# Float64 weights converted by VectorE alone, and a new order of the attention items behind each batch

## The chip, the cores and the metric

The kernel runs on one core of one Trainium2 chip. The metric is the device time of one execution in microseconds (us); the kernel before was timed three times. A core has five engines with a queue each: TensorE (PE, matmuls and transposes), VectorE (DVE), ScalarE (ACT), GpSimd (POOL) and SyncE (SP, which issues the DMAs). An engine works through its queue in order and waits on semaphores for what other engines and DMAs have to finish first.

## The reference

Three blocks in a row, for 8 batches, 576 tokens, width 512:

```python
def sm_attn(qq, kk, vv):                      # 8 heads of 64
    s = scale * np.matmul(qq, kk.transpose(0, 1, 3, 2))
    a = np.exp(s - np.max(s, axis=-1, keepdims=True))
    return np.matmul(a / (np.sum(a, axis=-1, keepdims=True) + 1e-09), vv)
p_packed = sm_attn(p, k, v)                   # 32 packed queries
x = sm_attn(q, p_packed, p_packed)            # heads joined to width 512
h = gelu_tanh(x @ w_in)                       # 512 -> 1024
u, v = h[..., :512], h[..., 512:]
v_s = np.einsum('ts,bsd->btd', w_sg, layer_norm(v) * g_ln) + b_sg
x = x + (u * v_s) @ w_out
# 4 experts of one head of 64 with causal softmax, the best 2 of 4 per token:
out = sum_over_chosen(w_e * (softmax(causal(x @ wq[e] @ (x @ wk[e]).T / 8)) @ (x @ wv[e]) @ wo[e]))
```

All is float32 but `w_in`, `w_sg` and `w_out`, which arrive as float64 and have to be made float32 by the kernel (a pair of 32-bit words per number).

## The kernel before, in words

The second packed softmax has only 32 columns per head, so its probabilities `a2` (256 columns and 576 tokens in two halves Q = 0, 1) stand for x, and the weights that follow are multiplied with the packed values once per batch (`wp` for `w_in`, `bdq` and `bdv` for the folded MoE weights). Products keep float32 accuracy by splitting both factors into a high and a low part (`a2h`, `a2l`; `wph`, `wpl`) and adding three products.

**The prologue** (about the first 125 us) loads and converts the weights (`from_f64`, L132), does the packed attention of batch 0 and folds `w_out` into the MoE weights (L257). A conversion handles 512 columns at a time: integer work on DVE (L137 to L139), the low word and the absolute value of the high word on ACT (L140, L141), a product and a sum on POOL (L142, L143), and the last select and product on DVE (L144). There are twelve such pieces: eight of `w_in` (two halves of four) and four of `w_out`. In the prologue a scheduler chooses the order of all engines.

**The main loop** takes about 112.7 us per batch. PE's order there is by hand, and only PE's: `front` holds the value tiles `v` (L519) and the gate tiles `u`, `back` the spatial products `vs` (L570), the MoE projections `qk` (L599, L604) and `vlog` (L629, L633), and, spread between them, the ten attention items of the batch before and the packed attention of the batch after. An item is a token tile and a pair of experts: S0 to S9 are its scores and softmax, T0 to T9 the transposes of the probabilities, y0 to y4 the products with the values, o0 to o4 the output tiles. S8 and S9 (`att_last`, L707 and L713) belong to the last 64 tokens and take two PSUM buffers each; T8 and T9 are at L744. The packed attention of the next batch goes through `pT`, `natT` (transposes of k and q, L326), `s` (L349; s1 is k against the packed queries, s2 is q against the packed values), `a1T`, `pp`, `ppT` (L401) and `split_a2` (L465 on ACT, L81 on POOL). A function `run` merges two lists of such steps by given costs. The other engines' orders follow from the scheduler's priorities.

PSUM has four buffers (`pd`), taken in turn: a product cannot start until the contents of the buffer four takes ago have been read by ACT or DVE. Of the buffers in SBUF the four of slot "C" matter here: `a2h` and `a2l` of the next batch take the places of those of this batch and so wait until the last `qk` product (L604) has read them.

Of the kernel before, what the change touches and what calls it, by code (L numbers as in the profile page):

```python
# [7 lines left out]
F32 = mybir.dt.float32  # L8
# [17 lines left out]
def packed_attention_mlp_moe_kernel(  # L26
# [39 lines left out]
    def slot(tag, dt=F32, w=None, name=None):  # L66
        t = sb.tile([P, BY[tag]], dt, tag=tag, name=name or ("s" + tag), bufs=NB[tag])
        return t if w is None else t[:, :w]
# [60 lines left out]
            nc.sync.dma_start(raw_in[f, j][64 * d:64 * d + 64],  # L129
                              src[j * P + 64 * a:j * P + 64 * a + 64, f * 1024:(f + 1) * 1024])  # L130

    def from_f64(raw, top, pw, dst):  # L132

        words = raw.rearrange("p (n t) -> p n t", t=2)
        lw, hw = words[:, :, 0], words[:, :, 1]
        low, in_range = lw.bitcast(F32), hw.bitcast(F32)
        nc.vector.tensor_scalar(top, hw, 3, 0x3FFFFFF8, op0=OP.logical_shift_left, op1=OP.bitwise_and)  # L137
        nc.vector.scalar_tensor_tensor(top, hw, -0x40000000, top, op0=OP.bitwise_and, op1=OP.bitwise_or)
        nc.vector.tensor_scalar(pw, top, -0x800000, None, op0=OP.bitwise_and)  # L139
        nc.scalar.activation(in_range, in_range, AF.Abs)  # L140
        nc.scalar.activation(low, lw.bitcast(U32), AF.Copy, scale=2.0 ** -52)  # L141
        nc.gpsimd.tensor_tensor(pw.bitcast(F32), low, pw.bitcast(F32), op=OP.mult)  # L142
        nc.gpsimd.tensor_tensor(pw.bitcast(F32), pw.bitcast(F32), top.bitcast(F32), op=OP.add)  # L143
        nc.vector.scalar_tensor_tensor(dst if dst is not None else low, in_range, LEAST_F64, pw.bitcast(F32),  # L144
                                       op0=OP.is_ge, op1=OP.mult)
        return low

    wst = {}

# [19 lines left out]

    def prep_w_in(f):  # L170
        t = w_tile(f"in{f}")
        for j in range(4):
            dst = t[:, j, :]
            from_f64(raw_in[f, j], dst.bitcast(I32), slot("t", I32, 512, name="pw"), dst)
        keep_w(f"in{f}")

    folded = {}
# [58 lines left out]
    def prep_w_out(c):  # L236

        wo = slot("p", w=512, name="wo")
        from_f64(raw_out[c], wo.bitcast(I32), slot("t", I32, 512, name="pw"), wo)
        pt = pd("woT")[:, 0, :]  # L240
        for j in range(4):
            nc.tensor.transpose(pt[:, j * P:(j + 1) * P], wo[:, j * P:(j + 1) * P], ident)
        t = slot("D", w=512, name="woT")
        act_copy(t, pt)
        woT[c] = t
# [50 lines left out]
    def p1_steps(b):  # L296
# [68 lines left out]
        def a1T(Q):  # L365
            a1 = s.pop(("a1", Q))
            pt = pd("a1T")[:, 0, :]
            for c in range(4):
                o = (c % 2) * HALF + (c // 2) * P
                nc.tensor.transpose(pt[:, c * P:(c + 1) * P], a1[:, o:o + P], ident)  # L370
            t = slot("t", w=512, name="a1t")
            nc.vector.tensor_copy(t, pt)
            r = small.tile([P, 2, 32], F32, name="a1r", bufs=1)
            for h in range(2):
                nc.vector.transpose(r[:, h, :], a1[:, h * HALF + 256:(h + 1) * HALF])
            s["a1T", Q] = (t, r)
# [80 lines left out]
    def split_a2(b, Q):  # L457
        s = ST[b]
        f = s.pop(("a2f", Q))
        hi, lo = slot("C", F32R, name="a2h"), slot("C", F32R, name="a2l")  # L460
        f = f.rearrange("p (a i) -> p i a", a=2)
        for o, i0, n in ((0, 0, S), (S, 256, 64)):
            src = f[:, i0:i0 + n // 2, :]
            dh, dl = (t[:, o:o + n].rearrange("p (i a) -> p i a", a=2) for t in (hi, lo))
            nc.scalar.activation(dh, src, AF.Copy)  # L465
            lo_part(nc.gpsimd, dl, src, dh)
        s["a2", Q] = (hi, lo)
# [44 lines left out]
    def v_tiles(b, cs):  # L512
        s = ST[b]
        pt2 = pd("v")
        for ci, c in enumerate(cs):
            n = 0
            for x, y in PASSES:
                for Q in range(2):
                    nc.tensor.matmul(pt2[:, ci, :], s["a2", Q][x][:, c * P:(c + 1) * P], wp_part(b, 1, y, Q),  # L519
                                     start=n == 0, stop=n == 5)  # L520
                    n += 1
        for ci, c in enumerate(cs):
            pt = pt2[:, ci, :]
            vg = slot("t", w=512, name="vg")
            nc.scalar.activation(vg, pt, AF.Gelu_apprx_tanh)
            st = small.tile([P, 6], F32, name="bnst")
            nc.vector.bn_stats(st, vg)
            mv = small.tile([P, 2], F32, name="mv")
            nc.vector.bn_aggr(mv, st)
            rstd = small.tile([P, 1], F32, name="rstd")  # L530
            nc.vector.tensor_scalar(rstd, mv[:, 1:2], LN_EPS, None, op0=OP.add)
            nc.gpsimd.tensor_tensor(rstd, rstd, mhalf, op=OP.pow)
            nc.vector.scalar_tensor_tensor(vg, vg, mv[:, 0:1], g_bc, op0=OP.subtract, op1=OP.mult)
            hi, lo = slot("B", F32R, 512, name="vnh"), slot("B", F32R, 512, name="vnl")
            nc.scalar.activation(hi, vg, AF.Copy, scale=rstd)
            if c < 4:
                nc.vector.scalar_tensor_tensor(lo, vg, rstd, hi.bitcast(F32), op0=OP.mult, op1=OP.subtract)
            else:
                nc.vector.scalar_tensor_tensor(hi[64:P], vg[64:P], rstd[64:P], hi[64:P].bitcast(F32),
                                               op0=OP.mult, op1=OP.subtract)  # L540
                nc.vector.memset(lo[64:P].bitcast(F32), 1.0)
                nc.scalar.activation(lo[:64], vg[:64], AF.Copy, scale=rstd[:64])
            s["vn", c] = (hi, lo)
# [4 lines left out]
    def u_tile(b, m):  # L548
        s = ST[b]
        u = slot("D", name="u")  # L550
        pt = pd("u")
        n = 0
        for x, y in PASSES:
            for Q in range(2):
                for h in range(2):
                    nc.tensor.matmul(pt[:, h, :HALF], wp_part(b, 0, y, Q)[:, m * P:(m + 1) * P],
                                     s["a2", Q][x][:, hs(h)], start=n == 0, stop=n == 5)
                n += 1
        nc.scalar.activation(two(u), pt[:, :, :HALF], AF.Gelu_apprx_tanh)
        s["u", m] = u  # L560
# [234 lines left out]
    def do(steps):  # L795
        for _, f in steps:
            f()
# [32 lines left out]
    def front(b, go):  # L830

        v_tiles(b, VT[0])
        v_tiles(b, VT[1])
        v_tiles(b, VT[2])
        go("T0")
        for m in range(4):
            u_tile(b, m)

    def back(b, go, extra=()):
        main = []  # L840

        def add(cost, fn, *a):
            main.append((cost, lambda: fn(*a)))

        go("S1")
        vs_tile(b, 0)
        go("T1 S3 y0")
        vs_tile(b, 1)
        go("T2 S5 o0 T3")
        vs_tile(b, 2)  # L850
        go("y1 T4 S6")
        vs_tile(b, 3)
        go("T5 o1 S7")
        bdw(b)
        weights(b + 1, ("in1", "in0"))
        nxt = attention(b)
        add(4.0, go, "y2 T6 S8")
        add(4.8, qk, b, 0)
        add(3.5, go, "T7 o2 S9")
        add(4.8, qk, b, 2)  # L860
        add(3.0, go, "y3 T8")
        add(2.7, go, "o3 T9")
        add(2.0, go, "y4")
        add(4.2, vlog, b, VT[0])
        add(1.0, go, "o4")
# [12 lines left out]
        nxt("S0 S2")
        if b + 1 == B:
            qk(b, 3)  # L880
            return nxt
        wp_mm(b + 1, 1)
        qk_mm(b, 3)
        wp_out(b + 1, 1)
        qk_out(b, 3)
        wprime(b + 1, 0)
        weights(b + 1, ("qk", "vg"))
        nxt("S4")
        return nxt

    P1 = {}
# [6 lines left out]

    first = p1_steps(0)
    do(first[:6])  # L900
    for j in range(4):
        load_raw_in(1, j)
    do(first[6:14])
    for c in range(4):
        load_w_out(c)
    for j in range(4):
# [26 lines left out]
    with tc.manual_schedule(engines={mybir.EngineType.PE}):  # L933
        ahead(1)
        go = back(0, attention(-1))
        for b in range(1, B):
            front(b, go)
            go = back(b, go)
        go("S4 S1 T0 S3 T1 y0 T2 S5 o0 T3 y1 T4 S6 o1 T5 S7 y2 T6 S8 o2 T7 S9 y3 T8 o3 T9 y4 o4")


# [29 lines left out]
```

## Time and profile before

| | |
|---|---|
| median of 3 runs | 1007.45 us (1006.8 to 1008.74) |
| profiled execution | 1005.63 us, span 1003.9 us |
| mean granted clock of TensorE | 0.948 |
| PE busy | 895.2 us, 89% |
| DVE / ACT / POOL busy | 57% / 47% / 12% |

PE is the busiest engine by far. Its busy time is a sum over 8009 matmul records, so the profile is read by the places at which PE stands still and by the stretches in which its granted clock is below 1.00: in the 40 slices of the page the clock is lowest in the second and third (0.7 and 0.5 of the full one), inside the prologue.

### The profile page before, as it was taken

The page shows a single profiled execution, that of the slowest core. Times are in us where ns is not written, and L with a number is a line of the kernel's source. Part 1 is how long each engine was busy: PE and PEld are TensorE (multiplying, and loading weights), DVE is VectorE, ACT ScalarE, POOL GpSimd, SP SyncE. Part 2 cuts the span into 40 slices and gives each one's busy share as a digit, 9 for nine tenths or more (in the row PEclk, how much of TensorE's full clock was granted, in tenths as well). Part 3 has the DMA queues.
Part 4 walks back from the last instruction along what each step waited for, and adds up shares of the span by engine and source line. Part 5 has one row for each costly group of instructions (what it writes and reads, how often), then busy time and mean ns, then how long its engine had stood idle before and what let it go on. Part 6 is the DMA issues. An engine that isn't in the chain of part 4 may idle for free.

```text
span 1003.9 us, 19707 instructions
## 1 busy us (share of the span) xinstructions
PE 895.2 (89%) x8009; PEld 747.2 (74%) x8009; DVE 568.5 (57%) x1354; ACT 475.8 (47%) x1087; POOL 119.9 (12%) x120
## 2 busy tenths in 40 slices
PE   3529899899998999899998999999989999899987
PEld 2205788697877888697877888787868788687965
DVE  3897433865367543865367543864377543865154
ACT  4423523465436452565436452655436452554245
POOL 0565010210012000210012000200012000200000
PEclk9758899999999999999999999999998999999989
DMA  8863133103230143103320132104320231100001
GB/s 234 201 205 131 43 114 119 65 11 124 94 95 22 46 143 92 64 12 124 101 88 22 55 137 90 64 12 142 98 93 2 77 107 40 64 11 23 17 11 37
DMA packets 60191, 81.07 MB, mean 81 GB/s; under 512 B 15107, under 2 KB 48387, under 8 KB 57029
## 3 DMA queue, kind: packets, MB, share of 16 engines
q1 hardware_dynamic: 60100, 79.81, 24.9%
q8 instruction: 63, 1.03, 0.4%
q14 instruction: 28, 0.22, 0.1%
HBM read 66.68 MB, written 13.12 MB: 79 GB/s over the span
## 4 chain that ended last, share of the span: by engine, by line
PE 54%; DVE 16%; ACT 7%; POOL 2%; issue 2%; POOLq 0%; ACTq 0%
PE vs L570 7%; PE o L774 6%; PE qk L599 5%; PE vlog L629 5%; PE v L519 5%; PE y L759 4%; PE aTp L731 3%; PE sc L684 3%; PE qk L604 3%; PE natT L326 3%; PE vlog L633 2%; DVE at L695 2%; ACT at L691 2%; PE sc L713 2%; DVE nm L687 2%
## 5 line engine op out<-in xcount | busy, mean ns | idle before, releaser
L599 PE MATMUL qk<-gh,w_qk 128*128 128x288 f32 x512 | 94.0, 306 | 2.1 <-DVE bdq L81 1.5
L691 ACT ACTIVATE at<-sc,nm 128x256 f32<-128x256 f32 (+3 forms) x128 | 66.1, 524 | 57.2 <-DVE nm L687 55.4
L570 PE MATMUL vs<-w_sg,vnh 128*128 128x288 f32 x512 | 91.7, 301 | 0.0
L599 PEld LDWEIGHTS qk<-gh,w_qk 128*128 128x128 f32 x512 | 76.5, 194 | 13.8 <-DVE nm L687 5.0
L78 ACT ACTIVATE aT<-aTp 128x512 f32<-128x512 f32 (+4 forms) x160 | 61.0, 436 | 52.5 <-PE aTp L731 47.3
L417 POOL TENSOR_TENSOR bt<-bt,mx 128x576 f32<-128x576 f32 x14 | 16.3, 1162 | 577.4 <-DVE gsm L662 531.6
L570 PEld LDWEIGHTS vs<-w_sg,vnh 128*128 128x128 f32 x512 | 74.5, 189 | 4.2 <-DVE yl L81 2.5
L629 PE MATMUL vlog<-w_vg,gh 128*128 128x260 f32 (+1 forms) x320 | 60.6, 287 | 0.0
L687 DVE TENSOR_REDUCE nm<-sc 128x2 f32<-128x256 f32 (+3 forms) x64 | 51.7, 819 | 12.3 <-PE sc L684 11.2
L759 PE MATMUL y<-aT,v 128*64 128x128 f32 (+2 forms) x960 | 58.1, 264 | 0.4 <-ACT aT L78 0.4
L695 DVE TENSOR_SCALAR at<-at,sm,gw 128x256 f32<-128x256 f32 (+3 forms) x128 | 55.9, 478 | 2.3
L599 PE MATMUL qk<-gl,w_qk 128*128 128x288 f32 x256 | 55.4, 298 | 0.0
L759 PEld LDWEIGHTS y<-aT,v 128*64 128x64 f32 (+1 forms) x960 | 46.9, 137 | 11.3 <-issue 5.4
L774 PE MATMUL o<-w_o,yh 128*128 128x512 f32 (+1 forms) x160 | 53.8, 418 | 1.4 <-ACT yh L762 1.4
L570 PE MATMUL vs<-w_sg,vnl 128*128 128x288 f32 x256 | 54.8, 295 | 0.0
L731 PE MATMUL aTp<-ident,at 128*128 128x128 f32 x320 | 47.9, 280 | 5.7 <-DVE at L695 5.7
L635 ACT ACTIVATE v<-vlog 128x512 f32<-128x512 f32 (+1 forms) x24 | 12.6, 524 | 83.4 <-PE vlog L633 83.4
L629 PEld LDWEIGHTS vlog<-w_vg,gh 128*128 128x128 f32 (+1 forms) x320 | 47.5, 178 | 2.2
L684 PE MATMUL sc<-qk 64*128 64x128 f32 (+3 forms) x384 | 47.6, 352 | 0.2 <-DVE qk L81 0.2
L731 PEld LDWEIGHTS aTp<-ident,at 128*128 128x128 f32 x320 | 37.5, 142 | 13.1 <-issue 7.0
L578 DVE TENSOR_TENSOR gt<-vs,u 128x576 f32<-128x576 f32 x32 | 24.1, 754 | 39.4 <-PE vs L575 39.4
L519 PE MATMUL v<-wph,a2h 128*128 128x512 f32 x80 | 32.2, 477 | 14.8 <-ACT a2h L465 14.8
(210 smaller groups left out, 2098.5 us busy)
## 6 DMA issues: line engine op xcount, KB each, us to landing
w_in<-kept_in SPq DMA_DIRECT2D x14, 1024.0 KB
k<-in_k_dram SPq DMA_DIRECT2D x32, 256.0 KB
v<-in_v_dram SPq DMA_DIRECT2D x32, 256.0 KB
q<-in_q_dram SPq DMA_DIRECT2D x32, 256.0 KB
w_qk<-kept_qk SPq DMA_DIRECT2D x8, 1024.0 KB
out_dram<-ot SPq DMA_DIRECT2D x32, 256.0 KB
w_vg<-kept_vg SPq DMA_DIRECT2D x8, 520.0 KB
raw_w_qk<-in_moe_w_in_dram SPq DMA_DIRECT2D x8, 256.0 KB
```

The costliest lines, as they stand in the source:

```text
L78: nc.scalar.activation(o, i, AF.Copy, scale=scale)
L519: nc.tensor.matmul(pt2[:, ci, :], s["a2", Q][x][:, c * P:(c + 1) * P], wp_part(b, 1, y, Q), start=n == 0, stop=n == 5)
L570: nc.tensor.matmul(pt[:, h, :HALF], s["vn", c][x][:, cols], w_sg[y][:, c, hs(h)], start=(c, x, y) == (0, 0, 0), stop=False)
L599: nc.tensor.matmul(o[:, h, :], W["w_qk"][y][:, m, cols], s["g", m][x][:, hs(h)], start=(m, x, y) == (0, 0, 0), stop=False)
L629: nc.tensor.matmul(pt[:n, ci, :260], s["g", m][x][:, c * P:c * P + n], W["w_vg"][y][:, m, :], start=(m, x, y) == (0, 0, 0), stop=False)
L684: nc.tensor.matmul(pt[:, e, :L], qs[x][r, j * P:L], ks[y][r, :L], start=False, stop=i == 2, skip_group_check=True)
L687: nc.vector.tensor_reduce(nm, pt[:, :, :L], axis=AX.X, op=OP.max, negate=True)
L691: nc.scalar.activation(ats[e][:, :L], pt[:, e, :L], AF.Exp, bias=nm[:, e:e + 1], accum_out=sm[:, e:e + 1])
L695: nc.vector.tensor_scalar(ats[e][:, :L], ats[e][:, :L], sm[:, e:e + 1], s["w"][:, j, 2 * pr + e:2 * pr + e + 1], op0=OP.mult, op1=OP.mult)
L731: nc.tensor.transpose(pt[:, e, c * P:c * P + P], ats[e][:, c * P:c * P + P], ident)
L759: nc.tensor.matmul(pt[64 * e:64 * e + 64, pr * w:pr * w + w], s["v2"][:m, c, col:col + D], s["aT", pr, e, j][c][:m, :], start=c == 0, stop ...
L774: nc.tensor.matmul(pt[:n, :], ys[x][:, pr * n:pr * n + n], W["w_o"][y][:, pr, :], start=i == 0, stop=i == 5)
```

## The change

It has three parts, and the order of PE's work is seen best in the rows further down.

- `from_f64` works on DVE alone, with seven instructions (L137 to L143 of the changed kernel). `w_in` is converted in pieces of 1024 columns, `w_out` in pieces of 512 as before. The scratch buffer `pw` of the wide pieces comes from slot "A".
- In the prologue the loads of q are put ahead of half of the raw `w_in`, those of v behind all of it, and batch 0 copies `a1T` by ACT.
- In the main loop S4 leaves the end of the batch and stands between o0 and y1; T1 goes behind the second `vs`, next to y0; S8 and S9 stand closer together behind the product of `qk` 0, whose evacuation comes after S8; `pp`, `ppT` and s2 of the next batch stand between the `vlog` tiles; `u` 0 goes ahead of T0. `split_a2` and the s2 step are issued under a higher priority of the scheduler.

```diff
-    def from_f64(raw, top, pw, dst):
+    def from_f64(raw, pw, dst):
...
-        low, in_range = lw.bitcast(F32), hw.bitcast(F32)
+        top, f, in_range = dst.bitcast(I32), pw.bitcast(F32), hw.bitcast(F32)
         nc.vector.tensor_scalar(top, hw, 3, 0x3FFFFFF8, op0=OP.logical_shift_left, op1=OP.bitwise_and)
         nc.vector.scalar_tensor_tensor(top, hw, -0x40000000, top, op0=OP.bitwise_and, op1=OP.bitwise_or)
         nc.vector.tensor_scalar(pw, top, -0x800000, None, op0=OP.bitwise_and)
-        nc.scalar.activation(in_range, in_range, AF.Abs)
-        nc.scalar.activation(low, lw.bitcast(U32), AF.Copy, scale=2.0 ** -52)
-        nc.gpsimd.tensor_tensor(pw.bitcast(F32), low, pw.bitcast(F32), op=OP.mult)
-        nc.gpsimd.tensor_tensor(pw.bitcast(F32), pw.bitcast(F32), top.bitcast(F32), op=OP.add)
-        nc.vector.scalar_tensor_tensor(dst if dst is not None else low, in_range, LEAST_F64, pw.bitcast(F32),
-                                       op0=OP.is_ge, op1=OP.mult)
-        return low
+        nc.vector.scalar_tensor_tensor(f, lw.bitcast(U32), 2.0 ** -52, f, op0=OP.mult, op1=OP.mult)
+        nc.vector.tensor_tensor(f, f, dst, op=OP.add)
+        nc.vector.tensor_scalar(hw, hw, 0x7FFFFFFF, None, op0=OP.bitwise_and)
+        nc.vector.scalar_tensor_tensor(dst, in_range, LEAST_F64, f, op0=OP.is_ge, op1=OP.mult)
...
-        go("T1 S3 y0")
+        go("S3")
         vs_tile(b, 1)
-        go("T2 S5 o0 T3")
+        go("T1 y0 T2 S5")
         vs_tile(b, 2)
-        go("y1 T4 S6")
+        go("T3 o0 S4 y1")
         vs_tile(b, 3)
-        go("T5 o1 S7")
+        go("T5 S6 o1 T4")
         bdw(b)
...
-        add(4.0, go, "y2 T6 S8")
-        add(4.8, qk, b, 0)
-        add(3.5, go, "T7 o2 S9")
+        qk_mm(b, 0)
+        go("y2 S7 S8")
+        qk_out(b, 0)
+        go("T6 S9")
+        add(2.0, go, "o2")
         add(4.8, qk, b, 2)
-        add(3.0, go, "y3 T8")
-        add(2.7, go, "o3 T9")
-        add(2.0, go, "y4")
+        add(2.9, go, "T7 y3")
+        add(2.2, go, "T8 o3")
+        add(3.1, go, "T9 y4")
         add(4.2, vlog, b, VT[0])
-        add(1.0, go, "o4")
-        add(4.2, vlog, b, VT[1])
-        add(2.1, vlog, b, VT[2])
-        add(0.0, gates, b)
...
-        for Q, (_, f) in enumerate(p1[cut:]):
-            f()
-            split_a2(b + 1, Q)
+        for Q in range(2):
+            if p1:
+                with tc.high_priority(offset=150):
+                    p1[cut + Q][1]()
+                    split_a2(b + 1, Q)
+            if Q == 0:
+                go("o4")
+                vlog(b, VT[1])
+        vlog(b, VT[2])
+        gates(b)
...
         weights(b + 1, ("qk", "vg"))
-        nxt("S4")
...
-        go("S4 S1 T0 S3 T1 y0 T2 S5 o0 T3 y1 T4 S6 o1 T5 S7 y2 T6 S8 o2 T7 S9 y3 T8 o3 T9 y4 o4")
+        go("T0 S1 S3 T1 y0 T2 S5 o0 T3 S4 y1 T5 S6 o1 T4 S7 y2 T6 S8 o2 T7 S9 y3 T8 o3 T9 y4 o4")
```

Three places in the instruction order follow. The first is PE from the last transposes of the packed values (`ppT`) to the first value product `v` of the next batch. Before:

```order
L633 MATMUL vlog<-bdv,a2l 64x260
L401 MATMUL ppT<-ident,pp_9788 128x128
L401 MATMUL ppT<-ident,pp_9865 128x128
L349 MATMUL s_9920<-qT,ppT 32x288 x8
L349 MATMUL s_9949<-qT,ppT 32x288 x8
...
L474 MATMUL wp<-w_in_9300,ppT 32x512 x8
...
L604 MATMUL qk<-a2l,bdq 128x288 x2
L474 MATMUL wp<-w_in_9302,ppT 32x512 x8
...
L684 MATMUL sc<-qk 128x384 x6
L519 MATMUL v<-wph,a2h 128x512 x2
```

After, from the same transposes (line numbers are three lower):

```order
L398 MATMUL ppT<-ident,pp_9703 128x128
L398 MATMUL ppT<-ident,pp_9772 128x128
L346 MATMUL s_9783<-qT,ppT 32x288 x8
...
L630 MATMUL vlog<-bdv,a2l 128x260
L346 MATMUL s_9861<-qT,ppT 32x288 x8
...
L630 MATMUL vlog<-bdv,a2l 64x260
...
L471 MATMUL wp<-w_in_9236,ppT 32x512 x8
...
L601 MATMUL qk<-a2l,bdq 128x288 x2
L471 MATMUL wp<-w_in_9238,ppT 32x512 x8
L516 MATMUL v<-wph,a2h 128x512 x2
```

The s2 products (`s<-qT,ppT`) moved from behind the last `vlog` tile to places between the tiles, and the scores of S4 (the 384 wide `sc`) no longer stand ahead of the first `v`.

The second place is PE from S8 to S9 of a batch (`sc` 64x288 x12 is one item; T6 and T7 are `aTp` x8). Before:

```order
L474 MATMUL bdv<-w_vg,ppT 32x260 x8
L759 MATMUL y<-aT,v_8314 64x128 x12
L731 MATMUL aTp<-ident,at 128x128 x8
...
L713 MATMUL sc<-qk 64x288 x12
L315 MATMUL pT<-ident,pn 128x128 x2
L326 MATMUL natT<-ident,k 128x128 x8
L328 MATMUL remT<-ident,kr 128x128
L599 MATMUL qk<-gh,w_qk_748 128x288 x2
...
L731 MATMUL aTp<-ident,at 128x128 x8
L774 MATMUL o<-w_o_948,yh 128x512
...
L713 MATMUL sc<-qk 64x288 x12
```

After:

```order
L601 MATMUL qk<-a2l,bdq 128x288 x2
L756 MATMUL y<-aT,v_8314 64x128 x12
...
L681 MATMUL sc<-qk 128x512 x6
...
L710 MATMUL sc<-qk 64x288 x12
L728 MATMUL aTp<-ident,at 128x128 x8
...
L710 MATMUL sc<-qk 64x288 x12
L771 MATMUL o<-w_o_904,yh 128x512
```

Between S8 and S9 there stood most of `qk`, a transpose of k, s1, T7 and o2; now T6 alone stands there, and the first product of `qk` 0 is ahead of both.

The third place is PE around s1 of the second half (Q = 1) and y3 (`y` x16 is y3). Before:

```order
L326 MATMUL natT<-ident,k 128x128 x8
L328 MATMUL remT<-ident,kr 128x128
L731 MATMUL aTp<-ident,at 128x128 x8
...
L604 MATMUL qk<-a2l,bdq 128x288 x2
L349 MATMUL s_9560<-kT,pT 32x288 x8
L326 MATMUL natT<-ident,q 128x128 x8
L328 MATMUL remT<-ident,qr 128x128
L759 MATMUL y<-aT,v_8314 64x128 x16
```

After:

```order
L323 MATMUL natT<-ident,k 128x128 x8
L325 MATMUL remT<-ident,kr 128x128
L346 MATMUL s_9503<-kT,pT 32x288 x8
L728 MATMUL aTp<-ident,at 128x128 x8
L756 MATMUL y<-aT,v_8314 64x128 x16
L323 MATMUL natT<-ident,q 128x128 x8
```

s1 of the second half now follows its own transposes of k directly, and y3 follows T7 directly, where two other steps stood in between.

## Rows read from the trace of the kernel before

**Rows 1.** Waits of PE from 130 us: total us, times, longest us.

```profile
PE v L519 <- ACT a2h L465: 14.8, 6, 2.5
PE sc L707 <- DVE yl L81: 8.6, 7, 1.2
PE sc L707 <- DVE bdq L81: 5.8, 7, 0.8
PE aTp L731 <- DVE at L695: 5.7, 8, 3.2
PE wp L474 <- DVE bt L411: 5.5, 6, 0.9
...
PE v L519 <- POOL a2l L81: 2.2, 5, 0.5
PE qk L599 <- DVE bdq L81: 1.5, 1, 1.5
```

**Rows 2.** Windows: us, busy us of PE, PEld, DVE, ACT, POOL, PEclk, DMA, GB/s.

```profile
406.00:411.00 5.00, 4.73 (x44) 3.92 (x44) 4.86 (x14) 3.32 (x10) 1.16 (x1) 1.00 0.47 162
420.00:425.00 5.00, 5.00 (x20) 4.07 (x19) 3.10 (x10) 2.07 (x4) 0.56 (x1) 0.82 0.00 0
465.00:470.00 5.00, 4.02 (x26) 3.33 (x26) 2.90 (x5) 2.96 (x7) 0.00 (x0) 0.66 0.65 237
685.00:690.00 5.00, 2.93 (x38) 2.38 (x39) 2.96 (x7) 3.69 (x10) 0.00 (x0) 1.00 0.90 324
```

**Rows 3.** Timeline of PE, a first v and an S8: start us, us, instruction.

```profile
419.43 1.06 PE L519 MATMUL v<-wph,a2h 128*128 128x512 f32 x2
...
421.91 0.62 PE L519 MATMUL v<-wph,a2h 128*128 128x512 f32 x2
...
466.31 1.70 PE L713 MATMUL sc<-qk 64*64 64x288 f32 x12
```

**Rows 4.** Timeline of POOL before the first v of that batch.

```profile
412.24 1.86 POOL L81 TENSOR_TENSOR a2l<-a2f,a2h 128x576 fp32r<-128x576 f32 x2 [2.55 <-ACT a2h L465]
```

**Rows 5.** Timeline of PE in the tail: y0 behind T1, S8, S9, y3.

```profile
969.89 0.86 PE L759 MATMUL y<-aT,v 128*64 128x128 f32 x4 [0.44 <-ACT aT L78]
...
985.29 1.00 PE L713 MATMUL sc<-qk 64*64 64x288 f32 x12
...
989.31 0.19 PE L707 MATMUL sc<-causal,identb 128*128 128x64 bf16 x1 [0.49 <-ACT at L719]
...
990.36 1.97 PE L759 MATMUL y<-aT,v 128*64 128x128 f32 x32
```

**Rows 6.** Timeline of ACT behind the transposes of k, Q = 1.

```profile
476.63 1.08 ACT L334 ACTIVATE kT<-natT 128x512 f32<-128x512 f32 x2 [1.02 <-PE natT L326]
477.61 0.75 ACT L358 ACTIVATE a<-s,st 128x576 f32<-128x576 f32 x1
```

**Rows 7.** Windows of the prologue, columns as in rows 2.

```profile
42.00:43.00 1.00, 0.21 (x1) 0.00 (x0) 1.00 (x4) 1.00 (x2) 0.00 (x0) 0.50 1.03 220
50.00:75.00 25.00, 5.44 (x22) 2.34 (x18) 24.45 (x30) 7.24 (x13) 16.73 (x13) 0.50 0.66 202
```

**Rows 8.** Timeline of DVE in the prologue.

```profile
42.55 0.38 DVE L139 TENSOR_SCALAR pw<-w_in 128x512 int32<-128x512 int32 x1
42.85 0.41 DVE L137 TENSOR_SCALAR w_in<-raw_w_sg 128x512 int32<-128x512 int32 x1
...
46.89 0.75 DVE L417 TENSOR_TENSOR bt<-bt,mx 128x576 f32<-128x576 f32 x1
...
48.84 0.68 DVE L138 SCALAR_TENSOR_TENSOR w_in<-raw_w_sg,w_in 128x512 int32<-128x512 int32 x1
...
51.14 1.48 DVE L139 TENSOR_SCALAR pw<-wo 128x512 int32<-128x512 int32 x1
```

**Rows 9.** Groups by line of DVE, prologue: busy us, mean ns, idle.

```profile
L139 DVE TENSOR_SCALAR pw<-w_in 128x512 int32<-128x512 int32 x8 | 7.4, 932 | 0.1
L144 DVE SCALAR_TENSOR_TENSOR w_in<-raw_w_sg,pw 128x512 f32<-128x512 f32 x4 | 5.8, 1491 | 2.7 <-POOL pw L143 2.7
```

More of the change, by code (lines that the diff above doesn't have):

```diff
@@ L171, in prep_w_in @@
         t = w_tile(f"in{f}")
-        for j in range(4):
-            dst = t[:, j, :]
-            from_f64(raw_in[f, j], dst.bitcast(I32), slot("t", I32, 512, name="pw"), dst)
+        for i in range(2):
+            from_f64(raw_hold[f][i][:, :2048], slot("A", I32, 1024, name="pw"),
+                     t[:, 2 * i:2 * i + 2, :].rearrange("p j n -> p (j n)"))
         keep_w(f"in{f}")
@@ L238, in prep_w_out @@
         wo = slot("p", w=512, name="wo")
-        from_f64(raw_out[c], wo.bitcast(I32), slot("t", I32, 512, name="pw"), wo)
+        from_f64(raw_out[c], slot("t", I32, 512, name="pw"), wo)
         pt = pd("woT")[:, 0, :]
@@ L371, in a1T @@
             t = slot("t", w=512, name="a1t")
-            nc.vector.tensor_copy(t, pt)
+            (nc.vector.tensor_copy if b else act_copy)(t, pt)
             r = small.tile([P, 2, 32], F32, name="a1r", bufs=1)
@@ L834, in front, with back @@
         v_tiles(b, VT[2])
+        u_tile(b, 0)
         go("T0")
-        for m in range(4):
+        for m in range(1, 4):
             u_tile(b, m)
-    def back(b, go, extra=()):
+    def back(b, go):
         main = []
@@ L900, in packed_attention_mlp_moe_kernel @@
     do(first[:6])
-    for j in range(4):
+    for j in range(2):
         load_raw_in(1, j)
-    do(first[6:14])
+    do(first[10:14])
+    for j in range(2, 4):
+        load_raw_in(1, j)
+    do(first[6:10])
     for c in range(4):
```

## The prediction

> **What bounds the kernel now.** PE is busy for 89% of the span, so I read first the waits of PE behind the prologue, then the windows in which its granted clock is under 1.00, then single places in the timeline, and last the prologue. The waits [rows 1] come back in every batch: the first value product `v` stands for `a2h` (14.8 us in 6 batches, up to 2.5) and then for `a2l` (2.2); S8 stands for PSUM buffers that hold `bdq` and `bdv` (8.6 and 5.8 in 7 batches); T1 for its probabilities (5.7, of which 3.2 in the tail); `wp` for s2's `bt` (5.5). The other engines are idle often enough; each wait is a short chain through ACT, DVE or POOL that PE reaches too early.
>
> A wait costs twice where the clock falls behind it. Behind the `a2h` wait the granted clock of the window is 0.82, behind one S8 it is 0.66, behind another S8 it stays 1.00 [rows 2]. In cycles this is one level against the other, 1.2 against 2.4 GHz: a pair of `v` products takes 1.06 us and then 0.62, S8's twelve matmuls 1.70 where the same ones in the tail take 1.00 [rows 3, 5]. The price of such a fall at `v`: from 419.43 to 421.91 are 2.48 us for three pairs that start 0.46 apart at full clock (estimate from 0.62 less the overlap of 0.16), so 2.48 - 1.38 = 1.1. At S8 it is 1.70 - 1.00 = 0.7. The trace has falls at all 6 `a2h` waits and, of the 7 S8, at 5.
>
> The prologue is another regime. From 50 to 75 us DVE is busy for 24.45 of 25 us and PE for 5.44 [rows 7]. There DVE decides when the weights are ready.
>
> **The change part by part.** Sums are made against the profiled execution, 1005.63 us, 1.73 above its span of 1003.9; the median of the runs is 1.8 above it.
>
> *1. s2 earlier, S4 gone from the end.* Both s2 now stand between the `vlog` tiles, the first some 9 us earlier than before, so that the chain `bt`, softmax, `a2f` is over long before `qk` 3 ends. The `wp` wait goes (5.5) and so do both `v` waits in their present form (14.8 + 2.2): 22.5 us. What is late next: `a2h` and `a2l` take the SBUF places that the last `qk` product has to release, and POOL then makes `a2l` of the first half in 1.86 [rows 4] before it starts the second. POOL started at 412.24; the large part of the second half (1.16, an estimate: the share of 1.86 that goes with 576 of the row's 576 and 64 columns, plus a fixed part) would be ready at 415.3. PE has the last `wp` (about 1.0) and two kinds of products to do from 412.2 on and wants it at about 414.4. So 0.9 stays, times 7 = 6.3. Gain 22.5 - 6.3 = 16.2. A stall of 0.9 is as long as the present `wp` wait, in whose window the clock stays 1.00 [rows 2], so I also count the clock, 6 x 1.1 = 6.6, of which I take 6.0 (one fall in eleven may stay). Bounds: nothing (the stall only moves) to 22.5 + 6.6 = 29.
>
> *2. S8 and S9.* S8 now comes when `bdq` and `bdv` have long been read, under `qk` 0. The 14.4 us go, with 5 x 0.7 = 3.5 of clock. Late next is S9, with only T6 in front of it. In the tail S8's matmuls begin at 985.29 and S9's second buffer is free at 989.31, after a wait of 0.49 in spite of o2 and T7 between [rows 5]: that is about 3.1 behind the last of S8's matmuls. T6 covers 1.1 of it, so S9 waits 2.0, 7 x 2.0 = 14.0, and if half of these waits also drop the clock, 7 / 2 x 0.7 = 2.5. Gain 17.9 - 16.5 = 1.4. Bounds: -10 (the exponentials of S8 stand behind the evacuation of `qk` 0 too) to +10.
>
> *3. T1 behind the second `vs`.* The steady part of its wait, 5.7 - 3.2 = 2.5, goes. But y0 follows T1 at once; the tail has that place, with 0.44 [rows 5]: 7 x 0.44 = 3.1. Net -0.6, bounds -3 and +2.5.
>
> *4. s1 of the second half directly behind its transposes.* ACT takes 1.08 for `kT` from the moment at which PE has finished them [rows 6]; T7 and o2 covered this, and now 7 x 1.1 = 7.7 is lost. Bounds 3 (the second of the two copies alone) and 11.
>
> *5. y3 directly behind T7.* ACT copies T7's result in two parts, 1.08 in all, and the exponential of s1 (0.75, and its sum read out) can stand between them [rows 6]. y3 takes 1.97 and its first half needs T6 alone [rows 5], which covers 0.98: 1.08 + 0.75 + 0.2 + 0.1 - 0.98 = 1.15, 6 batches, 6.9. y4 behind T9 is the smaller case, 6 x 0.25 = 1.5 (estimate: half of y0's). Together -8.4, bounds -13 and -2.
>
> *6. The first batch and the tail.* In the first batch there are no items between the steps of the packed attention; they follow each other at once and I count one `kT` and two exponentials, 2.6; its `qk` wait of 1.5 goes [rows 1]. In the tail the 3.2 of T1 goes with one fall of 1.1, and the scores of S1 with less in front of them give about 2 back (an estimate: its maximum and exponential as in a steady item, less one product): +2.3. Net +1.2, bounds -2 and +5.
>
> *7. Conversions.* The seven instructions cost per 512 columns 0.41 (as L137) + 0.68 (L138) + 0.38 (L139) + 0.68 + 0.67 (the sum: 0.75 x 512 / 576) + 0.41 + 0.68 = 3.9; the added three are 0.68 + 0.67 + 0.41 = 1.76, times 12 pieces = 21.1. What DVE gets back is the time it lost beside POOL: L139 took 0.38 at 42.55, with POOL idle, and 1.48 at 51.14 with POOL at work [rows 8]. On eight L139 that is 7.4 - 8 x 0.38 = 4.4 and on four L144 5.8 - 4 x 0.68 = 3.1 [rows 9], 7.5 on 12 of 48 instructions; at that rate all would give 30, and if the rest gave nothing, 7.5. So DVE's work changes by something between -9 and +14, and the pieces of 1024 save the start of four times seven instructions. With a value near the middle the last weight comes when it did, and the prologue costs 0.5 more: the folds and `v` behind it stay as they are. POOL and ACT, which lose 24 instructions each, were on this path only through DVE. The order of the loads moves SP's queue: q comes earlier and v of batch 0 later, both under conversion. Bounds -9 and +14 where PE follows DVE one to one.
>
> Whether POOL is the cause decides between these ends. The DMA queues were full at 42 to 43 us (share 1.03) while L139 was at its quick value, and less full (0.66) in the window of the slow one [rows 7], so the rows speak for POOL and against the loads. By the Trainium skill, GPSIMD Engine Reference, section 1 (Specifications), GpSimd shares its SBUF interfaces with VectorE and contends with instructions that use the two-port mode or have two SBUF inputs; by that all of DVE's slow instructions turn quick, the lower end is nearer, and the sum would be about 9 lower, 991. [...]
>
> Sum: 16.2 + 6.0 + 1.4 - 0.6 - 7.7 - 8.4 + 1.2 - 0.5 = 7.6. Span 1003.9 - 7.6 = 996.3, execution 998.0, and at the median's level 999.8. The other edits (`u` 0 ahead of T0, S4 between o0 and y1, `a1T` by ACT in batch 0) I cost at nothing: a spatial product or a whole gate tile stands in front of each step that needs them; without this cover one more exponential, 0.75 [rows 6], would show per batch, about 5.
>
> **The rivals.**
>
> *Larger gain.* The waits in 2, 4 and 5 are chains through ACT and DVE whose order may leave them shorter: S9 at 1.0, s1 at 0.5 and y3 at 0.5 save 7 + 4.2 + 3.9 = 15 and the 2.5 of clock: 999.8 - 17.5 = about 982; half of it gives 990. For: ACT is under half busy. Against: S9's wait in the tail is in the trace, with more cover.
>
> *The gain is eaten, no change.* `a2h` waits anyway since its place is free only with the last `qk` product, so the stall at `v` stays above 2 us and drops the clock: part 1's 22.2 shrink to the `wp` wait of 5.5 and as much again for the chain behind it, 11: 999.8 + 11 = 1011; half of it 1005. For: `a2h` of the first half was released by `qk` already before, and POOL follows it at 412.24 [rows 4]. Against: that half was ready by the time it was wanted; only the second wasn't.
>
> *Slower by the clock.* Each of the three new waits (S9, s1, y3) drops the clock, 20 places in place of the 3.5 counted, at 0.7 to 1.1 each: 16.5 x 0.7 = 12 to 18, so 1011 to 1017. It decides from about 15 falls. For: S8's two waits of 1.2 and 0.8 did it in 5 of 7. Against: waits of 0.9 at `wp` didn't.
>
> *Slower by the prologue.* A new instruction on DVE costs as much as the slow ones (1.48) although POOL is idle: two of them at 1 us more are 24 on a path that was full, of which some 12 remain: 1011. It decides from 10 us. That the conversion is not on the path at all has [rows 7] against it.
>
> **How the numbers follow.** Chances: forecast 0.45 (range of its own 993 to 1005), larger gain 0.20, eaten 0.15, slower by the clock 0.09, by the prologue 0.11. A measurement of this kernel tells about 0.2% from no change, that is 2 us: faster is below 1005.4, slower above 1009.5. Faster takes the first two whole and half of the third (and a rest of the last two): 0.73; slower 0.08 + 0.08 of the last two and 0.02 of the third: 0.18; the rest, 0.09, is the same. The range reaches from the middle of the larger gain to the lower end of the slower ones, 987 to 1011.
>
> **What would show it.** The lists of waits: no `wp` for `bt`, at most 1 us per batch of `v` for `a2l`, new waits of S9 near 2.0, of s1 and y3 near 1.1. The windows behind `v` at clock 1.00. In the prologue the masks near 0.4 to 0.7 throughout, and the folds where they were. I am wrong if `v` still stands for `a2h` over 2 us, if S9 or s1 stands much longer or not at all, or if the folds begin more than 5 us earlier or later.

## The result and the profile after

The changed kernel takes 981.61 us (median of 4) against 1007.12 for the kernel before (4); the ratio is 0.9744, 95% interval 0.9725 to 0.9762. The forecast was 999.8 with 987 to 1011: right in sign, but with a gain of 7.6 where 26 came. One execution of the changed kernel, the profiled one, ran at a mean granted clock of 0.65, took 1250.66 us and is left out of the ratio. Rows of the kernel after are from another profiled execution of the same kernel (981.41 us, span 979.7, clock 0.966), from a run whose ratio to before was 0.9742 (0.9718 to 0.9766).

The waits of PE behind the prologue in the kernel after, as in [rows 1] (total us, times, longest us):

```profile
PE v L516 <- POOL a2l L81: 6.7, 7, 1.0
PE y L756 <- ACT aT L78: 6.4, 13, 0.7
PE sc L704 <- ACT at L688: 4.7, 7, 0.7
PE ppT L398 <- DVE pp L392: 4.6, 7, 0.7
PE s L346 <- DVE kT L332: 4.5, 7, 0.6
PE sc L704 <- ACT at L716: 3.7, 7, 0.5
PE qk L596 <- ACT at L716: 2.2, 6, 0.4
PE aTp L728 <- DVE at L692: 1.5, 1, 1.5
...
```

The forecast's list has come true place by place: `wp` no longer waits for s2, `v` only for `a2l` and by 1.0, T1 only once, in the tail; s1, y3, y4 and S9 wait anew. But S9 waits less than forecast, and the clock is another one. The windows behind `v` and behind S8 and S9 of one batch, columns as in [rows 2]:

```profile
410.00:415.00 5.00, 4.24 (x19) 3.50 (x20) 2.65 (x7) 2.10 (x3) 1.00 (x2) 1.00 0.22 87
415.00:420.00 5.00, 5.00 (x35) 4.73 (x34) 4.70 (x11) 4.21 (x9) 2.57 (x3) 1.00 0.00 0
460.00:465.00 5.00, 3.80 (x36) 2.85 (x33) 4.27 (x10) 4.08 (x11) 0.00 (x0) 1.00 0.00 2
465.00:470.00 5.00, 4.65 (x34) 4.12 (x33) 2.80 (x10) 3.55 (x8) 0.00 (x0) 1.00 0.49 134
```

In the 5 us windows from 125 us on, the kernel before has a clock under 1.00 at six first `v` (one of them for twice as long), at six S8 and in the tail; the sum of (1 - clock) times the window is about 26.5 us. The kernel after has it in the tail alone, about 4.4. Two readings in the prediction were too quick. The S8 of [rows 2] whose window is at 1.00 was followed by a fall in the next window (0.66 from 690 to 695 us), so six S8 and not five had one. And [rows 1] name `yl` and `bdq` as what ended S8's two waits, not `bdq` and `bdv`; the 14.4 us are the same.

**One batch in both traces.** From one `bdq` to the next the kernel before takes 112.69 us (459.90 to 572.59), the kernel after 109.42 (450.46 to 559.88). With each group of PE rows counted from its start to the next start, less the wait ahead of the next, the difference of 3.27 splits thus:

| place | before | after | difference |
|---|---|---|---|
| `v`, its 30 matmul pairs | 8.85 | 7.21 | -1.64 |
| waits of `v` | 2.90 | 0.96 | -1.94 |
| wait of `wp` | 0.93 | 0.00 | -0.93 |
| S8 and S9, their matmuls | 2.57 | 1.87 | -0.70 |
| first transposes of k behind S8 (all `natT`) | 4.19 | 3.66 | -0.53 |
| waits of S8, S9 and of the `qk` behind | 2.07 | 1.55 | -0.52 |
| s1 and s2, with their waits | 2.42 | 3.66 | +1.24 |
| y0 to y4 with their waits | 6.73 | 8.55 | +1.82 |
| the rest | | | -0.07 |

### The profile page after: what moved, and what is told of

Its sections match the earlier page's. It is cut to its first block, busy times and chain, and to the rows that moved or that the text cites. A ratio compares the mean times of both kernels' runs of the same rounds, so it can differ in the third digit from the quotient of the medians.

```text
span 1248.9 us, 19590 instructions
## 1 busy us (share of the span) xinstructions
PE 1177.7 (94%) x8009; PEld 927.3 (74%) x8009; DVE 557.8 (45%) x1360; ACT 464.2 (37%) x1065; POOL 84.5 (7%) x96
## 4 chain that ended last, share of the span: by engine, by line
PE 89%; DVE 3%; DMA 3%; ACT 3%; issue 1%; SPq 1%; ACTq 0%; DVEq 0%
PE vs L567 12%; PE qk L596 12%; PE o L771 7%; PE vlog L626 7%; PE v L516 6%; PE u L553 6%; PE qk L601 6%; PE y L756 5%; PE sc L681 4%; PE aTp L728 4%; PE vlog L630 3%; PE natT L323 3%; PE fold L254 3%; PE s L346 2%; PE wp L471 2%; PE aTp L741 1%
## 5 line engine op out<-in xcount | busy, mean ns | idle before, releaser
L567 PE MATMUL vs<-w_sg,vnh 128*128 128x288 f32 x512 | 118.1, 364 | 0.0
L596 PE MATMUL qk<-gh,w_qk 128*128 128x288 f32 x512 | 117.6, 367 | 0.0
L596 PEld LDWEIGHTS qk<-gh,w_qk 128*128 128x128 f32 x512 | 95.1, 216 | 15.9 <-DVE nm L684 7.2
L567 PEld LDWEIGHTS vs<-w_sg,vnh 128*128 128x128 f32 x512 | 95.6, 219 | 6.3 <-issue 2.6
L688 ACT ACTIVATE at<-sc,nm 128x256 f32<-128x256 f32 (+3 forms) x128 | 66.3, 524 | 59.3 <-DVE nm L684 58.5
L756 PE MATMUL y<-aT,v 128*64 128x128 f32 (+2 forms) x960 | 80.8, 312 | 1.5 <-ACT aT L78 1.5
L626 PE MATMUL vlog<-w_vg,gh 128*128 128x260 f32 (+1 forms) x320 | 79.4, 346 | 0.0
L567 PE MATMUL vs<-w_sg,vnl 128*128 128x288 f32 x256 | 70.2, 363 | 0.0
L684 DVE TENSOR_REDUCE nm<-sc 128x2 f32<-128x256 f32 (+2 forms) x64 | 52.1, 822 | 27.7 <-PE sc L681 26.5
L601 PE MATMUL qk<-a2h,bdq 128*128 128x288 f32 x256 | 59.1, 359 | 0.0
L626 PE MATMUL vlog<-w_vg,gl 128*128 128x260 f32 (+1 forms) x160 | 55.2, 345 | 0.0
```

The costliest lines, as they stand in the source:

```text
L567: nc.tensor.matmul(pt[:, h, :HALF], s["vn", c][x][:, cols], w_sg[y][:, c, hs(h)], start=(c, x, y) == (0, 0, 0), stop=False)
L596: nc.tensor.matmul(o[:, h, :], W["w_qk"][y][:, m, cols], s["g", m][x][:, hs(h)], start=(m, x, y) == (0, 0, 0), stop=False)
L601: nc.tensor.matmul(o[:, h, :], s["bd", Q][y][:, cols], s["a2", Q][x][:, hs(h)], start=False, stop=(Q, x, y) == (1, 1, 0))
L626: nc.tensor.matmul(pt[:n, ci, :260], s["g", m][x][:, c * P:c * P + n], W["w_vg"][y][:, m, :], start=(m, x, y) == (0, 0, 0), stop=False)
L688: nc.scalar.activation(ats[e][:, :L], pt[:, e, :L], AF.Exp, bias=nm[:, e:e + 1], accum_out=sm[:, e:e + 1])
L756: nc.tensor.matmul(pt[64 * e:64 * e + 64, pr * w:pr * w + w], s["v2"][:m, c, col:col + D], s["aT", pr, e, j][c][:m, :], start=c == 0, stop ...
```

## The experiments

Each was timed beside the kernel before on the same chip; gains below are against that, or against the changed kernel's 980.4. Beside these runs the kernel before took 1006.1 to 1006.9, so a difference under 1 us between two of them says nothing.

**The changed kernel again.** No edit.

> The changed kernel once more, for a profile at the clock of its timed runs. If my list of new waits holds (S9 2.0, s1 of the second half 1.1, y3 1.1 per batch, about 32 us in all), the waits of PE behind the prologue stay above 35 us and the missing 18 us have come from the prologue. If the larger gain is in the main loop, these waits sum to under 20 us and the granted clock stays at 1.00 behind v and S8.

980.37 us. The list of waits sums to 37.5 us with its small rows, as the first case had it, but the clock stays at 1.00 behind `v` and S8, as the second had it; the prologue's share is the next run's to tell.

**The prologue alone.** Kernel before with `from_f64`, the 1024-wide pieces, the order of the loads and the `a1T` copy of the change.

```diff
-        nc.gpsimd.tensor_tensor(pw.bitcast(F32), low, pw.bitcast(F32), op=OP.mult)
+        nc.vector.scalar_tensor_tensor(f, lw.bitcast(U32), 2.0 ** -52, f, op0=OP.mult, op1=OP.mult)
...
```

> Kernel before with the prologue of the change alone (conversion by VectorE in seven instructions, w_in in pieces of 1024, the loads and a1T of batch 0). By my sum 0.5 us slower than before (1007.6). If the conversion is what I mis-sized, it is 8 to 20 us faster (987 to 999), because VectorE is quick throughout and the prologue shorter. If the main loop is what I mis-sized, within 2 us of before.

1006.62 us, ratio 1.0002 (0.9988 to 1.0016): no difference. **The main loop alone**, the changed kernel with the prologue of before:

> The changed kernel with the prologue of before: only the order of the main loop and the tail is new. By my sum 8 us faster than before (999). If the new waits are much smaller than I worked out, 18 to 26 us faster (981 to 989). If the prologue carries the surplus, 990 or more.

979.44 us, ratio 0.973 (0.9709 to 0.975). The whole gain is in the main loop and the tail.

**Part 1 alone.** Kernel before with s2 between the `vlog` tiles and S4 away from the end:

```diff
-        for Q, (_, f) in enumerate(p1[cut:]):
-            f()
-            split_a2(b + 1, Q)
+        for Q in range(2):
...
+                    p1[cut + Q][1]()
+                    split_a2(b + 1, Q)
+            if Q == 0:
+                go("o4")
+                vlog(b, VT[1])
+        vlog(b, VT[2])
...
-        go("T2 S5 o0 T3")
+        go("T2 S5 o0 S4 T3")
...
-        nxt("S4")
```

> Kernel before with part 1 alone: s2 between the vlog tiles with the higher priority, and S4 between o0 and T3 in place of the end of the batch. By my forecast (16.2 of waits, 6.0 of clock) 22 us faster than before, 984. By the comparison of one batch in the two traces (wp 0.93, the v waits 1.94 and the slow v 1.64 gone, 4.5 per batch) 30 us faster, about 976; then this part alone is worth more than the whole change. S8 keeps its waits of 2.1 and the low clock behind them.

985.62 us, ratio 0.9787 (0.9762 to 0.9813): 20.9 us faster, which is the forecast's 22 and not the 30. The 30 took one batch for all. In that batch the gain is 3.3 and not 4.5: with S4 gone from the end, the first `u` waits for T0's copies (0.64; 3.8 us in all, 6 times) and T1's wait grows from 0.17 to 0.41. The next batch of before (572.59 to 683.43) had no `a2h` wait and no fall at `v` to lose and gains 1.6, and the tail is 1.5 longer. The falls of the clock at `v` are all gone; those at S8 stay in five of seven batches. So the 22 is met with some luck: the clock at `v` gave more than forecast, and the waits of `u`, which the prediction put at nothing, took it back.

**Everything but part 1.** The changed kernel with s2 behind the last `vlog` tile and S4 at the end of the batch.

> The changed kernel with part 1 undone: s2 behind the last vlog tile, S4 at the end of the batch. By my forecast of parts 2 to 7 (1.4 - 0.6 - 7.7 - 8.4 + 1.2 - 0.5) 14.6 us slower than before, 1021. By the comparison of one batch (S8 to S9 1.85 faster, s1 1.2 and y3, y4 1.8 slower) 3 to 8 us slower than before, 1009 to 1014, and v keeps its waits and its low clock.

1012.68 us, ratio 1.006 (1.0034 to 1.0085): slower than before by 6, as the second case had it. The parts are not additive: 20.9 and -6.2 make 14.7, the change gives 26. Part 1 without `u` 0 ahead of T0 pays at `u` (3.8); the rest without part 1 pays too (`u` waits 4.1 for `v`'s results in batches that end with S4, and `y` 10.6 for T's copies in place of 6.4). Together neither does. Undone in the changed kernel, part 1 is thus worth 32 us, alone 21, where the sum had 22.2 for it.

**More cover for S9: o2 ahead of it.**

```diff
-        go("T6 S9")
-        add(2.0, go, "o2")
+        go("T6 o2 S9")
+        add(2.0, go, "")
```

> The changed kernel with o2 moved ahead of S9, nothing else. If S9's wait (0.68 and 0.52 per batch) is a fixed chain behind S8, o2's 1.45 covers it: 7 x 1.2 = 8 us faster than the changed kernel, 972. If ScalarE's copy of o2's result gets ahead of S8's exponentials, as in the tail of before, 0.5 of wait stays per batch: 976. If VectorE's scalings of S7 come ahead of S8's maxima, 1.0 more: no gain.

979.75 us: nothing gained, and by none of the reasons named. The waits of S9 are gone and stand at o2 and `qk` instead:

```profile
PE qk L596 <- ACT at L716: 5.0, 6, 0.8
PE o L771 <- ACT at L688: 4.8, 7, 0.7
```

The four PSUM buffers hold S7, both of S8 and T6. Whatever comes next needs S7's, and ACT has not finished the exponentials that read it (L688). The wait belongs to the buffer, not to S9.

**No cover for S9: T6 ahead of S8.**

```diff
-        go("y2 S7 S8")
+        go("y2 S7 T6 S8")
         qk_out(b, 0)
-        go("T6 S9")
+        go("S9")
```

> The changed kernel with T6 moved ahead of S8, so that S9 follows S8 directly. The wait of S9 grows by what T6 covered, from 1.2 to about 2.2 per batch: 7 us slower than the changed kernel, 987, if the clock stays at its level. If a wait of 2.2 drops the clock as that of S8 did, 1.2 more per batch: 995, with windows of 0.66 to 0.85 behind S9.

983.87 us, ratio 0.977 (0.9744 to 0.9796): 3.5 slower than the changed kernel, half of the first case, and no window of the loop under 1.00. T6 thus covers 0.5 per batch, not 1.1.

**Without the priority.** `with tc.high_priority(offset=150)` replaced by `if True`.

> The changed kernel without the higher priority of s2 and split_a2; PE's order is the same. If the place of s2 alone removed the v wait, no change (980). If the scheduler's priority did it, a2h and a2l come later on ScalarE and GpSimd, v waits 2 or more again: 990 to 1000.

980.04 us, with `v` waiting for `a2l` as before the edit (6.8 in all) and for `a2h` not at all: the place of s2 alone does it.

**y3 and y4 one step later**, by other costs for the merge:

```diff
-        add(2.9, go, "T7 y3")
+        add(1.9, go, "T7")
+        add(1.0, go, "y3")
...
-        add(3.1, go, "T9 y4")
+        add(2.1, go, "T9")
+        add(1.0, go, "y4")
```

> The changed kernel with y3 and y4 one step later: the transposes of q stand between T7 and y3, the second a1T between T9 and y4. By the prediction's 1.15 and 0.25 this is worth 6 x 1.15 + 6 x 0.25 = 8.4 us: 972. By the comparison of one batch (1.5 and 0.35) 11 us: 969. If the wait travels with the PSUM buffer to the next step, as S9's did in the run with o2 ahead of it, no change: 980.

974.38 us, ratio 0.968 (0.9654 to 0.9706): 6.0 faster than the changed kernel. 0.4 of wait stays at y3, now behind s1's exponential on ACT.

**And T7 ahead of s1** (`o2` at 1.7 in place of 2.0):

> The run with y3 and y4 later, and T7 between the second transposes of k and s1. By the prediction's 1.1 per batch another 7 x 1.1 = 7.7 us: about 962. If ScalarE has then to do kT, aT of T7 and s1's exponential in a row that y3 waits for, less than half of it: 967.

965.6 us, ratio 0.9597 (0.9571 to 0.9623): 8.8 more. The terms of the forecast for s1, y3 and y4 were 7.7 and 8.4, 16.1 together; taking these waits away gave 14.8.

**S7 back ahead of `bdq`.**

```diff
-        go("T5 S6 o1 T4")
+        go("T5 S6 o1 T4 S7")
...
-        go("y2 S7 S8")
+        go("y2 S8")
```

> The changed kernel with S7 back ahead of bdq, as in the kernel before, S8 and S9 where they are. If S9 waits because VectorE and ScalarE have S7 to finish before S8, the waits of 0.68 and 0.52 and that of qk (0.3) go: 7 x 1.5 = 10 us faster than the changed kernel, 970. If S9 waits for S8 itself, by the 3.1 of the tail less T6, nothing is gained: 980. If bdq now waits for S6's buffer as long, 980 too, with that wait in the list.

975.12 us, ratio 0.9681 (0.9648 to 0.9713). It gains 5.3, half of the first case. The wait of 0.68 goes, 0.64 and `qk`'s 0.35 stay: S9 waited for S7 with half of its wait, for S8 with the other.

**Both covers.**

> The run with y3, y4 and s1 covered, together with S7 ahead of bdq. If the waits are independent the gains add: 965.6 less 6 x 0.84 (109.45 to 108.6 per batch), about 960.5. If they share a buffer, between 962 and 966.

961.22 us, ratio 0.9546 (0.9533 to 0.9558): the gains add, and this version beats both kernels. Its list of waits has only `a2l`, `ppT`, S9's second buffer and `qk` left in every batch:

```profile
PE v L516 <- POOL a2l L81: 6.7, 7, 1.0
PE ppT L398 <- DVE pp L392: 4.6, 7, 0.7
PE sc L704 <- ACT at L716: 4.5, 7, 0.6
PE qk L596 <- ACT at L716: 2.2, 6, 0.4
```

**S7, S8 and S9 back in their places of before, all else as changed.**

```diff
-        qk_mm(b, 0)
-        go("y2 S7 S8")
-        qk_out(b, 0)
-        go("T6 S9")
-        add(2.0, go, "o2")
+        go("y2 T6 S8")
+        qk(b, 0)
+        add(2.0, go, "o2 S9")
```

with S7 behind T4.

> The changed kernel with S7, S8 and S9 back where they were against qk 0: S7 ahead of bdq, S8 behind T6 and ahead of qk 0, S9 behind o2. By my forecast part 2 is worth 1.4 us: 982. By the comparison of one batch (2.07 of waits and about 1.2 of low clock at S8 against 1.20 and 0.35 at S9) it is worth 1.7 per batch, 12 us: 992, with windows of 0.66 to 0.9 behind S8. If S9 ahead of o2 was cheap only because S8 had come early, S9 waits too, and more than 992.

987.28 us, ratio 0.9811 (0.9797 to 0.9825): part 2 is worth 6.9 here, five times the forecast and between the first two cases. The clock fell behind three of the seven S8, in these windows:

```profile
345.00:350.00 5.00, 3.65 (x24) 2.74 (x22) 3.42 (x7) 1.99 (x5) 0.00 (x0) 0.71 0.76 292
350.00:355.00 5.00, 5.00 (x36) 4.91 (x35) 1.30 (x5) 1.83 (x5) 0.00 (x0) 0.95 0.02 8
565.00:570.00 5.00, 2.96 (x25) 2.02 (x23) 2.88 (x8) 3.05 (x8) 0.00 (x0) 0.89 0.94 388
570.00:575.00 5.00, 5.00 (x30) 5.00 (x31) 2.45 (x6) 1.76 (x4) 0.00 (x0) 0.77 0.02 8
680.00:685.00 5.00, 5.00 (x32) 4.78 (x32) 2.61 (x7) 1.76 (x4) 0.00 (x0) 0.66 0.31 126
```

The batches with such a fall take 111.42, 111.46 and 111.52 us, those without 109.96 to 110.00: one fall costs 1.5. The waits ahead of S8 without the fall cost 0.5 per batch more than the changed kernel's 109.45. They are the same in all seven batches, with a fall (first) and without one, by the timeline of PE:

```profile
344.35 1.09 PE L728 MATMUL aTp<-ident,at 128*128 128x128 f32 x8 [0.68 <-ACT at L688]
346.39 0.20 PE L704 MATMUL sc<-causal,identb 128*128 128x64 bf16 x1 [0.95 <-DVE bdq L81]
346.99 0.19 PE L704 MATMUL sc<-causal,identb 128*128 128x64 bf16 x1 [0.40 <-DVE bdv L81]
347.11 1.70 PE L710 MATMUL sc<-qk 64*64 64x288 f32 x12
...
455.78 1.09 PE L728 MATMUL aTp<-ident,at 128*128 128x128 f32 x8 [0.69 <-ACT at L688]
457.82 0.20 PE L704 MATMUL sc<-causal,identb 128*128 128x64 bf16 x1 [0.95 <-DVE bdq L81]
458.42 0.19 PE L704 MATMUL sc<-causal,identb 128*128 128x64 bf16 x1 [0.40 <-DVE bdv L81]
458.54 1.00 PE L710 MATMUL sc<-qk 64*64 64x288 f32 x12
```

## Why the prediction was wrong

**Right, by place and size.** The prologue: forecast -0.5, measured none (ratio 1.0002). The seven instructions took what the rows gave, 0.68 for the new product at 512 columns and 1.22 at 1024, 0.42 for the mask. (Only `w_in` and `w_out` arrive as float64, `w_sg` is float32; `raw_w_sg` in these rows is a place that holds raw `w_in`, `raw_w_vg` and `raw_w_o` hold raw `w_out`.)

The timeline of DVE in the prologue of the kernel after, and of POOL at the same time:

```profile
38.44 0.42 DVE L142 TENSOR_SCALAR raw_w_vg<-raw_w_vg 128x512 int32<-128x512 int32 x1
...
46.35 0.68 DVE L140 SCALAR_TENSOR_TENSOR pw<-raw_w_vg,pw 128x512 f32<-128x512 uint32 x1
...
58.53 1.22 DVE L140 SCALAR_TENSOR_TENSOR pw<-raw_w_sg,pw 128x1024 f32<-128x1024 uint32 x1
...
71.67 2.03 DVE L140 SCALAR_TENSOR_TENSOR pw<-raw_w_o,pw 128x512 f32<-128x512 uint32 x1
```

```profile
71.39 2.51 POOL L81 TENSOR_TENSOR a2l<-a2f,a2h 128x576 fp32r<-128x576 f32 x2 [69.68 <-ACT a2h L462]
```

One of them took 2.03 in place of 0.68, at a moment at which GpSimd made `a2l`. The Trainium skill states that GpSimd contends with VectorE's instructions that have two SBUF inputs (GPSIMD Engine Reference, section 1, Specifications); this one has two, and the 2.03 agrees. The mask over every second word took 0.42, as L137 with its 0.41 on the same stride [rows 8]. The others shown, with GpSimd idle, are quick, as the prediction's lower end had it, and yet the time is not 9 us lower. One reason shows in the trace: the order of the loads is new as well, and between 5 and 77 us DVE stands for loads for 15.5 us in place of 9.8. No run has the conversion without the loads, so what it is worth alone stays open. The last piece of `w_out` was ready for PE at 76.99 (76.43 before), and the first `vs` started at 124.70 (124.61).

Part 1's wait: the first `v` behind the last `wp`, and the stall for `a2l`, in the timeline of PE after (start us, us, instruction, wait ahead of it):

```profile
407.37 1.09 PE L471 MATMUL wp<-w_in,ppT 64*32 64x512 f32 x16
408.39 0.72 PE L516 MATMUL v<-wph,a2h 128*128 128x512 f32 x2
...
410.76 0.50 PE L516 MATMUL v<-wph,a2l 128*128 128x512 f32 x1 [0.96 <-POOL a2l L81]
```

Forecast 0.9, measured 0.96, after 3.69 us of POOL for both halves. s1 was put at 1.1 per batch and took 1.05: 0.64 in the list of waits and 0.41 inside the group of its matmuls (1.13 in place of 0.72), since ACT's second copy of `kT` ends while they run. The other 0.2 of the table's 1.24 is s2, whose two halves now stand apart. y0, y3 and y4 were put at 0.44 + 1.15 + 0.25 = 1.84 per batch and took 1.82. The runs that covered y3 with y4, and then s1, gave 6.0 and 8.8.

**Right by luck: the tail.** It gained 2.4 (from the last `bdq` to the last matmul 89.95 before, 87.53 after) where 2.3 stood, but not by the terms of that sum. T1's wait there shrank from 3.2 to 1.5 and did not go, the fall of the clock behind it stayed (the slowest window has 0.52 before and 0.50 after), the scores of S1 wait 0.9 and not 2, and the stretch holds an S8 and an S9 whose gain the forecast had counted in part 2.

**Wrong: part 2, and the clock in parts 1 and 2.** Part 2 was put at 1.4: 14.4 of waits and 3.5 of clock against 14.0 and 2.5. The prediction had the right places here, and three sizes failed.

- S9's wait of 2.0. It was taken from the tail [rows 5], 3.1 behind S8's last matmul. In the kernel after it is 2.5, by the timeline of PE around S8 and S9:

```profile
458.57 0.96 PE L681 MATMUL sc<-qk 64*128 64x512 f32 x6
...
459.62 1.00 PE L710 MATMUL sc<-qk 64*64 64x288 f32 x12
460.56 1.09 PE L728 MATMUL aTp<-ident,at 128*128 128x128 f32 x8
462.33 0.19 PE L704 MATMUL sc<-causal,identb 128*128 128x64 bf16 x1 [0.68 <-ACT at L688]
463.04 0.19 PE L704 MATMUL sc<-causal,identb 128*128 128x64 bf16 x1 [0.52 <-ACT at L716]
```

S8's matmuls start at 459.62 and end some 0.94 later, S9's second buffer is free at 463.04; T6 (1.1) and S9's own first product (0.2) fill part of that and leave 0.68 + 0.52 = 1.2. DVE works in another order than in the tail. There it scaled S7's probabilities before it took S8's maxima, in the kernel after it takes the maxima first. Tail of before, then after, DVE:

```profile
986.51 1.00 DVE L695 TENSOR_SCALAR at<-at,sm,gw 128x512 f32<-128x512 f32 x2
987.43 1.41 DVE L718 TENSOR_REDUCE st<-sc 64x1 f32<-64x576 f32 x2
```

```profile
459.57 1.23 DVE L684 TENSOR_REDUCE nm<-sc 128x2 f32<-128x1024 f32 x1 [0.20 <-PE sc L681]
460.71 1.40 DVE L715 TENSOR_REDUCE st<-sc 64x1 f32<-64x576 f32 x2
...
462.72 1.00 DVE L692 TENSOR_SCALAR at<-at,sm,gw 128x512 f32<-128x512 f32 x2
```

The row I took had 1.00 us of another item's work in it, which PE's rows alone do not show. The maxima begin 0.15 behind S8's matmuls in place of 1.2; some 0.4 of that is lost again, since ACT has S7's exponentials to do first, up to 462.2; it is these that the run with S7 ahead of `bdq` takes out of the way. 7 x (2.0 - 1.2) = 5.6 us, less 2.2 at the `qk` behind, is 3.4.

- A fall for every second S9. There was none in the loop, also not with 2.0 us of waits spread over S9 and the transposes behind it (the run without cover). 2.5 us.

- The price of a fall. I had 0.7 at S8, from its own matmuls; the transposes of k behind it are slow as well, so that it is 0.70 + 0.53 = 1.2 by the table, and 1.5 by the batches with and without a fall in the last run. At `v` I had 1.1, from three pairs alone; the 30 pairs together take 8.85 or 7.21, so 1.64. The trace of before could have told: its batch from 572.59 has no `a2h` wait and no fall, and there the pairs take 7.4. The pair that took 1.06 in [rows 3] took, at the same place of that batch:

```profile
642.25 0.63 PE L519 MATMUL v<-wph,a2h 128*128 128x512 f32 x2
```

With six falls at each place, one of those at `v` double, that is an estimated 6 x 1.2 to 1.5 + 7 x 1.64 = 19 to 20 us at stake, where the sum had 6.0 + 3.5 - 2.5 = 7.0. With the 3.4 of S9 these 12 to 13 us make up most of the 18 that were missing; what the rest is, the first batch and small groups among it, is not shown.

The rival "larger gain" came to 982, and by luck: of its shorter waits only S9's came (1.2, it had 1.0), s1 and y3 are as long as forecast, and the clock gave what these did not. The rival "slower by the clock" is refuted by the windows above, "eaten" by the 0.96 at `v`, and "by the prologue" by its ratio. What stays open is what decides whether the clock falls behind a wait. With the order of the last run 0.68 at T6 and 0.95 and 0.40 at S8 dropped it in three batches of seven; 0.24 and 1.15 at S9 and 0.65 behind it, in the run without cover, dropped it in none.

## What to carry to other kernels

Price a fall of the clock over all rows until the next one at full speed, best by two batches of which one has it, not by the first slow instruction; here a fall added 1.2 to 1.64 us to stalls of 2.1 (S8) and 2.9 (`v`). Before a row is taken as the price of a wait elsewhere, look at what the engine that ends it did in between there. And a step with more cover gains nothing where the wait belongs to a buffer that any step behind it needs: then the work that empties the buffer has to come earlier.

## What was not expected of the hardware

The same prologue ran at two clocks. Windows of the kernel after, then of the run with S7 to S9 back (us, busy us of PE, clock, DMA share, GB/s):

```profile
25.00:50.00 25.00, 10.55 (x146) 0.58 0.88 216
50.00:75.00 25.00, 2.20 (x8) 0.50 0.57 166
```

```profile
25.00:50.00 25.00, 10.97 (x148) 1.00 0.83 217
50.00:75.00 25.00, 3.29 (x12) 1.00 0.62 191
```

TensorE at twice the clock for 50 us was of little use: the first `bdq` came at 138.23 in place of 139.66, and with the same prologue at the lower clock it came at 137.90 in one run (T7 ahead of s1) and at 140.92 in another (S7 ahead of `bdq`). DVE is busy for all 25 us from 50 to 75 in both executions and sets the pace there. So the mean clock of an execution, 0.991 for the one and 0.966 for the other, says nothing of which is faster: the first took 987.28 us, the second 981.41.
